# One store of 128 partitions in place of two of 64, in a fused attention and mixture-layer kernel

## The chip, the core and the metric

The kernel runs on one core of a Trainium2 chip. The metric is device time in microseconds (us), the median of several executions. Beside the times there is one profiled execution with its trace, from which all durations below are taken. The names of the engines are those of the profile: PE is the matrix engine, PEld its weight loads, DVE, ACT and POOL the vector, scalar and general engines, SP an engine that only issues transfers (DMAs). "SPq", "ACTq" and "POOLq" are the queues from which transfers are issued.

## The reference

Two layers follow each other; both work on float32.

```python
# attention without softmax, 8 batches, 8 heads, 576 tokens, 64 wide
kv  = einsum('bhsd,bhse->bhde', k, v)
o   = einsum('bhsd,bhde->bhse', q, kv)
o   = o / sqrt(mean(o * o, axis=-1) + 1e-6) * g_norm
x   = o.transpose(0, 2, 1, 3).reshape(8 * 576, 512)      # 4608 tokens

# feed-forward, 512 -> 1024 -> 512
h    = x @ w_in
u    = h * softmax(h, axis=-1)
ln   = (u - mean(u)) / sqrt(var(u) + 1e-6) * g_ln         # over the 1024
out  = ln @ w_out                                         # 4608 x 512 float32
```

The output is 4608 rows of 512 float32, which is 2 KB a row and 9.44 MB in all.

## The kernel before

**Tokens.** The kernel counts the 576 tokens of a batch as 9p + j, with p from 0 to 63 and j from 0 to 8. A chunk is 512 tokens. Chunk c (0 to 7) holds j = 0 to 7 of batch c, and the ninth chunk, number 8 (`LAST`), holds j = 8 of all eight batches. A result of 128 tokens is one block m (0 to 3) of a chunk: two values of j, each with its 64 values of p. So block m of chunk c stands in an SBUF tile of 128 partitions, where partitions 0 to 63 belong to one j and 64 to 127 to another, and in memory its rows are two runs of 64 rows, each with a step of nine rows. The step between the two runs is two rows. For the ninth chunk all 128 rows of a block have the same step of nine rows.

**Stages of a chunk.** `kv_mm` (L369) forms k^T v of a batch. `o_mm` (L434) multiplies it with the turned q. For chunks 0 to 4 PE turns q (L416), and for chunks 5 to 8 a transposing DMA on the SP queue does it (`q_turn`, L425, tile `qT_sb`). ACT and DVE then form the normalised x (L521). `h` is x times w_in, on PE: L574 for chunks 0 to 3 and L603 for chunks 4 to 8, in which the tokens lie along the partitions. ACT takes the exponential, DVE forms u. For chunks 4 to 8 u is turned by two transposing DMAs per chunk, each for two blocks, again on the SP queue (`ht_turn`, L639, tile `w_sb`). `out_mm` (L751) multiplies with w_out into a PSUM bank of 128 x 512, `scale` (L757) multiplies by the reciprocal deviation into the tile `ob_sb` on DVE (L244) or ACT (L242), and `store` (L762) writes `ob_sb` to memory.

**The store.** For chunks 0 to 7, `store` issues two transfers for a block, one for each half of the partitions (L769): 64 partitions of 2 KB, 128 KB each. For the ninth chunk it issues one transfer of 128 partitions for a block, and two of half the columns for the last block (L765). The stores of chunks 0 to 7 are all issued from SP. Those of the ninth chunk come from ACT and SP.

**Buffers and order.** The order of all the work is written out by hand in `ORDER` (L20); each engine runs its own part of it in that order. There are four `ob_sb` buffers in rotation (`kept`, L209), so the scale of a block waits until the store of the block four before it has landed. On SP the order from 57 us on is the stores of chunk 0, the qT transpose of chunk 5, the stores of chunk 1, that of chunk 6, the stores of chunk 2, that of chunk 7, and then stores mixed with the ten `w_sb` transposes. Loads of q, k, v and the weights are issued from POOL (all that have the kind "software_dynamic" in the profile), except for the first three and three short rows of norm weights (L297, L299: one of 8 rows, two of one row), which SP issues. Every transfer from SP or ACT also signals one of eight semaphores in turn, and waits until the transfer that used it before has landed.

Of the kernel before, what the change touches and what calls it, by code (L numbers as in the profile page):

```python
# [177 lines left out]
def kernel(  # L178
# [14 lines left out]
    B, H, S, D = q.shape  # L193
# [35 lines left out]
    on = {"act": nc.scalar, "dve": nc.vector, "pool": nc.gpsimd, "sp": nc.sync}  # L229
# [426 lines left out]
    for c in [c for c in range(NC) if c not in TOKS]:  # L656
        for f in range(NF):
# [9 lines left out]
            if f % 4 == 3 and c in PAIRED:  # L667
                m = f // 4
# [93 lines left out]
    def store(engine, c, m, cols):  # L762
        t = T["ob", c, m]
        if c == LAST:
            on[engine].dma_start(out.rearrange("(r j) d -> j r d", j=9)[8, 128 * m:128 * m + 128, cols], t[:, cols])  # L765
            return
        for x in range(2):
            j = 2 * (2 * (m % 2) + x) + m // 2
            on[engine].dma_start(  # L769
                out[c * S:c * S + S, :].rearrange("(p j) d -> j p d", j=9)[j], t[64 * x:64 * x + 64, :]  # L770
            )

    all_cols = slice(0, d_model)
    for c in range(NC):
        for m in range(4):
            key = ("out", c, m)
            if (c, m) == (LAST, 3):
                for x in range(2):
                    cols, half = slice(x * d_model // 2, (x + 1) * d_model // 2), (*key, x)
                    add(("out", c, m, x), "pe", lambda _, half=half, cols=cols: out_mm(half, range(NF), cols),  # L780
                        [("w_center", f) for f in range(NF)] + ([("turnu", c, m // 2)] if c in TOKS else [("u", c, f) for f in range(NF)]),
                        [("w" if c in TOKS else "u", c), half])
                    add(("ob", c, m, x), "dve|act", lambda e, half=half, cols=cols: scale(e, half, cols),
                        [("out", c, m, x), ("rstd", c)], [half, ("ob", c, m), ("rstd", c)])
                    add(("store", c, m, x), "sp|act", lambda e, c=c, m=m, cols=cols: store(e, c, m, cols), [("ob", c, m, x)], [("ob", c, m)])
                continue
            n_parts = 4 if c == 0 else 2
            for part in range(n_parts):
                fs = range(part * NF // n_parts, (part + 1) * NF // n_parts)
                add(("out", c, m, part), "pe", lambda _, key=key, fs=fs: out_mm(key, fs, all_cols),  # L790
                    [("w_center", f) for f in fs] + ([("turnu", c, m // 2)] if c in TOKS else [("u", c, f) for f in fs])
                    + ([("out", c, m, part - 1)] if part else []), [("w" if c in TOKS else "u", c), key])
            add(("ob", c, m), "dve|act", lambda e, key=key: scale(e, key, all_cols), [("out", c, m, n_parts - 1), ("rstd", c)], [key, ("ob", c, m), ("rstd", c)])
            add(("store", c, m), "sp|act" if c == LAST else "sp", lambda e, c=c, m=m: store(e, c, m, all_cols), [("ob", c, m)], [("ob", c, m)])
# [54 lines left out]
```

## Time and profile before

| what | value |
|---|---|
| median of 3 executions | 187.71 us (187.10 to 187.97) |
| the profiled execution's own time | 188.43 us |
| its span on the core | 186.7 us |
| PE busy | 171.0 us (92%) |
| ACT busy | 143.7 us (77%) |
| DVE busy | 134.9 us (72%) |
| POOL busy | 73.2 us (39%) |
| queue of the POOL loads (q0), share of 16 DMA engines | 50.2% |
| queue of the SP transfers (q1), share of 16 DMA engines | 43.0% |
| stores of L769 | 64 issues, 0.59 us each on SP (median), first at 56.9 us, last at 179.6 us |
| granted clock of PE | 0.997 |

The span runs from the first to the last instruction of the core; the execution's own time is 1.7 us more. The queues' shares add up the time that each packet took over all 16 DMA engines. A DMA engine can have packets of two queues in hand at once, so the shares of a stretch can add up to more than one. "Idle" is only of interest on the engine or queue that ends last in its stage.

### The profile page before, as it was taken

How to read it: one execution, taken by the hardware profiler on the slowest of the kernel's cores; microseconds unless marked ns; L12 is line 12 of the kernel's file. 1: busy time of each engine (PE TensorE's matmuls, PEld its weight loads, DVE VectorE, ACT ScalarE, POOL GpSimd, SP SyncE). 2: the span in 40 equal slices, each digit the busy share in tenths (PEclk: the TensorE clock that was granted, in tenths of full speed). 3: DMA queues.
4: the chain of work that ended last, by engine and by line, in shares of the span. 5: the costliest groups of instructions: out<-in, count | busy, mean ns of one | idle time of the engine just before them, and what ended most of it. 6: DMA issues, size and time to landing. Idle time of an engine off the chain costs nothing.

```text
span 186.7 us, 4938 instructions
## 1 busy us (share of the span) xinstructions
PE 171.0 (92%) x1985; PEld 84.6 (45%) x2007; DVE 134.9 (72%) x280; ACT 143.7 (77%) x282; POOL 73.2 (39%) x88
## 2 busy tenths in 40 slices
PE   7968899799999999999967899999999999999890
PEld 5455354255454464444523454444444444444350
DVE  1035567998648976878448968999898899999500
ACT  2437899889788999899968799898989869572351
POOL 7743049998599693998970200000000000000000
PEclk9999999999999999999999999999999999999998
DMA  5999999999999999939969974965979672959994
GB/s 203 284 207 210 207 338 283 210 205 209 208 210 206 274 236 150 205 66 163 222 178 137 285 135 87 202 135 112 210 151 191 122 177 59 211 124 199 188 237 168
DMA packets 50139, 35.48 MB, mean 190 GB/s; under 512 B 31548, under 2 KB 43332, under 8 KB 50116
## 3 DMA queue, kind: packets, MB, share of 16 engines
q0 software_dynamic: 13552, 16.42, 50.2%
q1 hardware_dynamic: 36132, 18.10, 43.0%
q10 hardware_dynamic: 432, 0.66, 1.0%
q8 instruction: 15, 0.25, 0.5%
q14 instruction: 8, 0.07, 0.1%
HBM read 32.51 MB, written 9.44 MB: 225 GB/s over the span
## 4 chain that ended last, share of the span: by engine, by line
PE 55%; DMA 26%; POOL 6%; ACT 4%; DVE 3%; issue 3%; SPq 1%; ACTq 0%; POOLq 0%
PE out_ps L751 25%; PE h_ps L603 13%; DMA w_in_sb<-in_moe_w_in_dram 8%; PE h_ps L574 7%; DMA q_sb<-in_q_dram 5%; DMA v_sb<-in_v_dram 5%; DMA qT_sb<-q_sb 4%; DMA w_sb<-u_sb 3%; PE s_ps L501 3%; PE misc_ps L685 2%; ACT e_sb L581 2%; PE o_ps L443 2%; PE misc_ps L378 2%; PE misc_ps L416 2%; DMA out_dram<-ob_sb 1%
## 5 line engine op out<-in xcount | busy, mean ns | idle before, releaser
L603 PE MATMUL h_ps<-w_in_sb,x_sb 128*128 128x512 bf16 x153 | 37.8, 379 | 0.5 <-issue 0.2
L751 PE MATMUL out_ps<-w_out_sb,w_sb 128*128 128x512 bf16 (+1 forms) x166 | 37.3, 369 | 0.6 <-DMA w_sb<-u_sb 0.4
L611 ACT ACTIVATE e_sb<-h_ps,zero_t 128x512 f32<-128x512 f32 x40 | 27.2, 682 | 8.2 <-PE h_ps L603 7.6
L521 DVE SCALAR_TENSOR_TENSOR x_sb<-o_ps,g_cols,rst_sb 128x512 bf16<-128x512 f32 x36 | 26.5, 746 | 9.2 <-ACT rst_sb L509 7.6
L751 PE MATMUL out_ps<-w_out_sb,u_sb 128*128 128x512 bf16 x122 | 30.8, 379 | 2.0 <-ACT lss_sb L505 1.7
L574 PE MATMUL h_ps<-x_sb,w_in_sb 128*128 128x512 bf16 x122 | 31.2, 380 | 1.4 <-DMA w_in_sb<-in_moe_w_in_dram 0.5
L238 POOL TENSOR_TENSOR usq_sb<-u_sb 128x512 bf16<-128x512 bf16 x27 | 27.4, 1040 | 9.7 <-DVE u_sb L585 9.7
L617 DVE TENSOR_TENSOR u_sb<-h_ps,e_sb 128x512 bf16<-128x512 f32 x40 | 26.8, 683 | 2.0 <-ACT e_sb L611 1.8
L623 DVE BATCH_NORM_STATS2 bn_sb<-u_sb 128x6 f32<-128x512 bf16 x40 | 26.6, 685 | 0.4
L236 ACT ACTIVATE osq_sb<-o_ps,zero_t 128x512 bf16<-128x512 f32 x36 | 23.2, 688 | 4.3 <-PE o_ps L443 4.1
L585 DVE TENSOR_TENSOR u_sb<-h_ps,e_sb 128x512 bf16<-128x512 f32 x32 | 21.4, 687 | 6.5 <-ACT e_sb L581 6.2
L505 ACT ACTIVATE lss_sb<-s_ps,eps_t 128x512 f32<-128x512 f32 x32 | 21.9, 688 | 4.0 <-PE s_ps L501 3.7
L751 PEld LDWEIGHTS <-w_sb 128*128 128x128 bf16 x168 | 16.1, 98 | 19.1 <-DMA w_sb<-u_sb 1.5
L603 PEld LDWEIGHTS <-x_sb 128*128 128x128 bf16 x160 | 15.3, 98 | 18.7 <-issue 0.4
L509 ACT ACTIVATE rst_sb<-lss_sb,zero_t 128x512 f32<-128x512 f32 x32 | 23.0, 722 | 0.6
L581 ACT ACTIVATE e_sb<-h_ps,zero_t 128x512 f32<-128x512 f32 x32 | 21.3, 689 | 2.7 <-PE h_ps L574 2.5
L598 POOL TENSOR_TENSOR es_sb<-e_sb 128x512 bf16<-128x512 f32 x16 | 20.2, 1276 | 5.5 <-ACT e_sb L581 5.3
L242 ACT ACTIVATE ob_sb<-out_ps,rstd_sb 128x512 f32<-128x512 f32 (+1 forms) x18 | 11.6, 661 | 10.3 <-PE out_ps L751 5.8
L751 PEld LDWEIGHTS <-u_sb 128*128 128x128 bf16 x128 | 12.1, 98 | 15.8 <-issue 2.5
L574 PEld LDWEIGHTS <-w_in_sb 128*128 128x128 bf16 x128 | 11.3, 97 | 15.7 <-issue 2.7
L244 DVE TENSOR_SCALAR ob_sb<-out_ps,rstd_sb 128x512 f32<-128x512 f32 x19 | 14.0, 744 | 5.2 <-ACT rstd_sb L708 2.0
L501 PE MATMUL s_ps<-osq_sb,head_mean 128*128 128x512 bf16 x35 | 13.1, 380 | 0.5 <-DVE u_sb L585 0.3
(72 smaller groups left out, 159.6 us busy)
## 6 DMA issues: line engine op xcount, KB each, us to landing
out_dram<-ob_sb SPq DMA_DIRECT2D x65, 128.0 KB, 2.7
k_sb<-in_k_dram POOLq DMA_DIRECT2D x6, 576.0 KB, 10.2
v_sb<-in_v_dram POOLq DMA_DIRECT2D x6, 576.0 KB, 10.6
q_sb<-in_q_dram POOLq DMA_DIRECT2D x6, 576.0 KB, 10.7
w_sb<-in_moe_w_out_dram POOLq DMA_DIRECT2D x2, 1024.0 KB, 15.5
w_in_sb<-in_moe_w_in_dram POOLq DMA_DIRECT2D x2, 512.0 KB, 13.9
v_sb<-in_v_dram POOLq DMA_DIRECT2D x3, 288.0 KB, 11.2
q_sb<-in_q_dram POOLq DMA_DIRECT2D x3, 288.0 KB, 10.5
```

What stands on the lines that cost most here:

```text
L236: nc.scalar.activation(out=dst, in_=src, func=AF.Square, bias=zero_t[:, :])
L238: on[engine].tensor_tensor(out=dst, in0=src, in1=src, op=MUL)
L505: nc.scalar.activation(out=t[:, :], in_=T["s", i][:, :], func=AF.Ln, bias=eps_t[:, :])
L509: nc.scalar.activation(out=t.rearrange("p a b c -> p (a b c)"), in_=T["lss", i][:, :], func=AF.Exp, scale=-0.5, bias=zero_t[:, :])
L521: nc.vector.scalar_tensor_tensor(out=t[:, 2 * hf:2 * hf + 2, z], in0=T["o", c, hf, z][:, :, :, :], scalar=g_rep, in1=T["rst", (c, hf, z)][ ...
L574: nc.tensor.matmul(bank(("h", c, f), [128, 512])[:, :], w_in_sb[:, dt, f * 128:(f + 1) * 128], T["x", c][:, dt].rearrange("p a b c -> p (a ...
L581: nc.scalar.activation(out=t[:, f % 2, :], in_=T["h", c, f][:, :], func=AF.Exp, bias=zero_t[:, :])
L603: nc.tensor.matmul(bank(("h", c, m, g), [128, 512])[:, :], x[:, NP * (m ^ 2 * odd(c, dt)) + dt, :] if c in TOKA else x[:, dt, m // 2 ^ odd ...
L611: nc.scalar.activation(out=t[:, g, :], in_=T["h", c, m, g][:, :], func=AF.Exp, bias=zero_t[:, :], accum_out=se[:, m, g:g + 1])
L617: nc.vector.tensor_tensor(out=t[:, m, g * 512:(g + 1) * 512], in0=T["h", c, m, g][:, :], in1=T["e", c, m][:, g, :], op=MUL)
L623: nc.vector.bn_stats(out=t[:, m, g, :], in_=T["u", c][:, m, g * 512:(g + 1) * 512])
L751: nc.tensor.matmul(bank(key, [128, d_model])[:, cols], T["w", c][:, m, f, :] if c in TOKS else T["u", c][:, f, m * 128:(m + 1) * 128], w_o ...
```

## The change

For chunks 0 to 7, `store` issues one transfer of all 128 partitions of `ob_sb` for a block. The target is described with three dimensions: two runs (step of two rows), 64 rows (step of nine rows), and 512 columns. The two transfers of 64 partitions are gone. The same bytes go to the same places, in rows of 2 KB as before.

```diff
         if c == LAST:
             on[engine].dma_start(out.rearrange("(r j) d -> j r d", j=9)[8, 128 * m:128 * m + 128, cols], t[:, cols])
             return
-        for x in range(2):
-            j = 2 * (2 * (m % 2) + x) + m // 2
-            on[engine].dma_start(
-                out[c * S:c * S + S, :].rearrange("(p j) d -> j p d", j=9)[j], t[64 * x:64 * x + 64, :]
-            )
+        first = 4 * (m % 2) + m // 2
+        on[engine].dma_start(out[c * S:c * S + S, :].rearrange("(p j) d -> j p d", j=9)[first:first + 3:2], t[:, :])
```

In the built program SP has 32 transfers with the pattern 2x64x512 on the side of the target (and 128 rows of 512 on the side of the tile) where it had 64 of 64x512 on both sides. The order of the work on PE, DVE, ACT and POOL is the same. The eight semaphores are handed round over 32 fewer transfers, so some instructions wait on a semaphore of another number, and the scale of a block waits for one store where it waited for two.

## The prediction

> **What bounds the kernel now.** I read the page first: busy time, queues, and the chain that ended last.
>
> ```profile
> span 186.7 us, 4938 instructions
> PE 171.0 (92%) x1985; PEld 84.6 (45%) x2007; DVE 134.9 (72%) x280; ACT 143.7 (77%) x282; POOL 73.2 (39%) x88
> ...
> q0 software_dynamic: 13552, 16.42, 50.2%
> q1 hardware_dynamic: 36132, 18.10, 43.0%
> ...
> PE 55%; DMA 26%; POOL 6%; ACT 4%; DVE 3%; issue 3%; SPq 1%; ACTq 0%; POOLq 0%
> ```
>
> PE bounds: 92% busy and over half of the chain. The stores are hardly on it. In the chain in order of time they appear in two places: two issues ahead of a transpose, and the last ones, for whose buffers ACT waits.
>
> ```profile
> 116.83 0.45 SPq L769
> 117.28 0.05 issue
> 117.33 0.59 SPq L769
> 117.92 0.05 issue
> 117.97 5.40 DMA w_sb<-u_sb
> ...
> 176.57 0.38 SPq L769
> 177.01 0.59 SPq L769
> 177.69 0.55 SPq L769
> 178.29 2.59 DMA out_dram<-ob_sb
> ```
>
> So stores are cheap as long as 16 DMA engines share them. How many share one is the question here, and the queue view, asked by stretch, answers it for three shapes. From 0 to 57 us, ahead of the first store's packets, SP's queue has moved three loads of 128 rows in two runs (256 packets each), one of 8 rows and two of one row:
>
> ```profile
> q1 hardware_dynamic: 836, 1.77, 9.0%
> ```
>
> 836 = 3 x (256 + 16) + (8 + 8) + 2 x (1 + 1): a completion record from each of 16 engines for the 128 rows, from 8 for the 8 rows, from one for the single row, although that row has 64 elements that could have been split. From 57 to 70 us the same queue has only the eight half stores of chunk 0:
>
> ```profile
> q1 hardware_dynamic: 640, 1.05, 25.1%
> ```
>
> 640 = 8 x (64 + 16): 64 rows go over 16 engines, four rows each. In every row the outermost dimension is what gets shared out, and an engine takes no part if that dimension has nothing for it.
>
> **The change part by part.** *Sharing out.* The 32 new transfers have 128 rows on the tile's side and 2x64x512 on the target's. The outermost dimension of the target has two entries. No row of before has sides that differ, so the bounds are 16 engines (the tile's side decides) and 2 (the target's side). I take 2, as the row of one row of 64 elements is nearest: what lies inside the outermost dimension was not split to fill engines. The Trainium skill, page "DMA: Bandwidth & Descriptors", section "Why a DMA increments its semaphore by 16 and not by 1", states the same: the number of engines is the largest up to 16 that divides the slowest dimension of both sides, here 2. The trace agrees for 128, 64, 8 and 1. The same page's section "Rules for kernel authors" also says that two transfers on the two halves of the partitions should be one of 128 partitions; that speaks for the change, and by it alone the time would be that of the first rival below.
>
> *Price of a store on two engines.* Each carries 64 packets of 2 KB, 131 KB. Prices of an engine, from the queue view: the ninth chunk's stores from ACT (128 partitions, all engines), 175 to 186.7 us; the half stores with no other traffic, 150 to 155 us; one `w_sb` transpose, 110 to 115 us; in that order:
>
> ```profile
> q10 hardware_dynamic: 432, 0.66, 15.7%
> ...
> q1 hardware_dynamic: 493, 0.81, 74.0%
> ...
> q1 hardware_dynamic: 2080, 0.52, 54.3%
> ```
>
> The first: 0.157 x 16 x 11.7 = 29.4 us for 0.66 MB, 22 GB/s an engine, 5.9 us for 131 KB; 1 KB packets and completions are in that, and its 2 KB packets alone have a median of 84 ns in the trace, 64 x 84 = 5.4 us. The second: 0.740 x 16 x 5 = 59.2 us for 0.81 MB, 13.7 GB/s, 9.6 us (148 ns a packet). Beside loads the same half stores ran at 0.251 x 16 x 13 = 52.2 us for 1.05 MB, 20 GB/s. So 148 ns appears where all 16 engines read the same 64 partitions at once; taken as pairs in each other's way it is 74 ns each, 4.7 us a store, the low bound. With two engines, each on its own half, the ninth chunk's row is nearest: 5.4 us; bounds 4.7 and 9.6. A half store now holds an engine for 4 x 84 to 4 x 148 = 0.3 to 0.6 us.
>
> *Sum on one of the two engines, from the first store at 57 us.* Stores: 32 x 5.4 = 172.8. Transposes, all after 57 us and on all engines: 0.543 x 5 = 2.7 us for one of 16 blocks; ten of `w_sb` and one of `q_last` are 29.7, three of 18 blocks are 3 x 3.05 = 9.2; together 38.9. Loads: from 57 us to the end q0 has 25.7% of 129.7 us = 33.3 us of packet time per engine; in 57 to 80 us packet times overlapped to a share of 1.15, so 29. Ninth chunk: 1.05 MB over 16 engines, 32 packets x 84 = 2.7. Sum 243.4, so the two engines are through at 300.4, where the whole kernel ends at 186.7 now. This work was hidden behind PE, which has some 120 us of its own in that time; it is no cover any more.
>
> *Does the queue stay full?* Loads and stores share the engine packet by packet: four stores of chunk 0 (21.6) and the loads up to q of chunk 5 (three queued and five still to be issued, 8 x 2.8 = 22: one is 576 KB, at the 208 GB/s of the page's slices around 45 us) fill 57 to about 101 us. That load landed at 82.7 before (SP issued the transpose then), so qT of chunk 5 is some 20 us late; PE, which follows its order, waits at `kv_mm` and `o_mm`. SP issues in order: stores of chunk 1 behind that transpose, 104 to 126; qT of chunk 6 (before 95.0), about 129; stores of chunk 2 to about 154 with the last loads; qT of chunk 7 (before 105.5) and the first `w_sb` transpose (before 110.1) at about 157; and so on, each transpose behind up to four stores, 22 us. A block's scale (0.74 us) needs the store four before it landed; while three others still hold the engine for 16 us, the next is ready in time. So I let the queue run without gaps, at nothing. If each of the 14 transposes left it dry for the 1.8 us from issue to first packet (2.4 to landing, less 0.6 of packets), that would be 25 us; and if SP's waits for q loads (26.6 us before) were not filled, 27 more.
>
> *The end.* The last scale waits for chunk 7's last store to land: two halves 0.84, issue 0.45, landing 2.5 = 3.8 us. Span 304.2.
>
> *SP's issues.* 32 fewer of 0.59 us take 19 us off SP, worth nothing while the engines are the queue; in the chain shown they would be worth about one 0.59 before the transpose and one at the end. No other engine's order moves, and no load.
>
> Span 304.2 plus the 1.7 us outside it is 306; the profiled execution is 0.7 us above the median of the runs, so **305 us**.
>
> **The rivals.** *First, the other side: all 16 engines take part.* Then there are 8 packets an engine at 84 ns (0.67) for two halves of 4 x 148 (1.18). The chain gains 0.6 at the transpose at 117 us, 0.6 of issue and 0.5 of packets at the end: 188.4 - 1.7 = 186.7, against the median 186.0. It decides if the tile's 128 rows, not the target's 2 runs, are what is shared out. For it: 128 rows went over 16 engines in the loads, whose tile side looks the same. Against: their memory side began with 128 too.
>
> *Second, two engines at the slow pace:* 32 x (9.6 - 5.4) = 134 more, 439. Against: two engines on separate halves have no partner on their partitions.
>
> *Third, two engines, but a lone engine overlaps its packets,* so that 84 ns is twice what it costs: 32 x 2.7 = 86 less, 219. Against: from 2 to 5 us SP's loads fill 96.5% of 16 engines at 1.06 MB, 22.9 GB/s an engine, so packets of one queue follow each other, not over each other. Up to 1.15 of overlap with the loads and transposes is inside my range.
>
> *Fourth, two engines with gaps:* 305 + 25 = 330, or 357 with the unfilled waits.
>
> **How the numbers follow.** The forecast with smaller or larger gaps (254 to 357) has 0.78, the first rival 0.11 (0.08 faster, 0.02 within 0.5%, 0.01 slower), the second 0.05, the third 0.06. Low end: 4.7 us a store takes 22 off, 283; overlap of 1.15 on what is left takes (283 - 57) x 0.13 = 29 more, 254. High end: the fourth rival, 357. Faster 0.08, same 0.02, slower 0.90; 0.5%, or 0.9 us, is about what this kernel's times can tell.
>
> **What would show it.** Packets: 32 x (128 + 2) = 4160 of stores instead of 64 x 80 = 5120, so some 960 fewer than 50139 with two engines; 32 x 144 = 4608 and 512 fewer with sixteen. The median landing of a store rises from 2.7 us to 15 to 24. The chain turns from PE to DMA `out_dram` and `w_sb`, PE's busy time stays near 171 us of a longer span, and the DMA share from 110 us on falls to some 0.3, since 14 engines have only transposes. The step "two engines" is wrong if the landing stays under 4 us; the price is wrong if stores follow each other at other than 5.4 us; "no gaps" is wrong if the DMA view has stretches with nothing in hand.

## The result, and the profile after

The changed kernel takes 298.61 us (median of four executions, 298.24 to 299.15) against 187.41 us of the kernel before on the same chip (187.08 to 187.97): a ratio of 1.593, 95% interval 1.588 to 1.598. The profiled execution took 298.44 us, of which the span is 296.0. Some executions of five of the experiments below ran slower, at a lower granted clock of PE, and are left out of the times; for the kernel with stores from POOL that leaves one execution, and the trace is of a slower one.

The packets of the page before, and the head of the page of the changed kernel, with the granted clock of PE and the busy share of the DMA engines in 40 slices, the two queues with their packets, megabytes and share of 16 engines, and the chain that ended last:

```profile
DMA packets 50139, 35.48 MB, mean 190 GB/s; under 512 B 31548, under 2 KB 43332, under 8 KB 50116
```

```profile
span 296.0 us, 4893 instructions
PE 193.8 (65%) x1985; PEld 89.7 (30%) x2007; DVE 135.9 (46%) x280; ACT 144.0 (49%) x282; POOL 73.3 (25%) x88
...
PEclk9999999999857599859966959989977968557955
DMA  7999999997919333971585939769611961983221
...
DMA packets 49178, 35.47 MB, mean 120 GB/s; under 512 B 30588, under 2 KB 42372, under 8 KB 49156
q1 hardware_dynamic: 35172, 18.09, 41.3%
q0 software_dynamic: 13552, 16.42, 33.1%
...
DMA 63%; PE 17%; SPq 7%; ACT 4%; DVE 3%; POOL 2%; issue 2%; DVEq 0%; POOLq 0%; ACTq 0%
```

The bound has moved from PE to the transfers. PE is idle for a third of the span, and the chain is 63% DMA, the larger part of it `out_dram`. The other engines have their busy times of before; that of PE rose, to which the part on the prediction comes back. The packets say how the stores are shared out: 50139 - 49178 = 961 fewer. Two engines per store make 32 x (64 x 2 + 2) = 4160 records where there were 64 x (64 + 16) = 5120, 960 fewer; sixteen would have made 512 fewer. In queue 1 alone, which carries these stores, it is 36132 - 35172 = 960; the other packet is one of queue 14, which has no stores.

Where the time is lost shows in the chain in order of time. The pieces of 8 us and more from 57 us on, with their start and duration:

```profile
69.31 29.64 DMA out_dram<-ob_sb
...
104.43 25.16 DMA out_dram<-ob_sb
...
146.51 8.06 SPq L425
...
158.22 13.96 DMA w_sb<-u_sb
...
177.32 13.05 DMA qT_sb<-q_last
...
194.80 12.48 DMA out_dram<-ob_sb
...
210.33 28.35 DMA out_dram<-ob_sb x2
...
242.13 17.37 DMA out_dram<-ob_sb
...
267.12 24.85 DMA out_dram<-ob_sb x2
```

A piece of `out_dram` runs from the issue of a store to its landing ("x2" joins two); 25 to 30 us of it is a store that lands behind the others of its group. The transposes between them (`w_sb`, `qT_sb`) are in the chain with 13 to 14 us, where the first `w_sb` transpose in the chain of before has 5.4: they stand behind stores. "SPq L425" is the issue of a transpose that holds SP, with 8 us of it in the chain.

The queue view of a stretch in which only stores run, 215 to 225 us (GB/s of the core in 40 slices, then packets and queue 1):

```profile
GB/s 49 49 49 57 49 49 57 49 49 49 49 49 57 49 49 57 49 49 49 49 57 49 49 57 49 49 49 49 57 49 49 57 49 49 49 49 57 49 49 57
DMA packets 254, 0.51 MB, mean 51 GB/s; under 512 B 4, under 2 KB 4, under 8 KB 254
...
q1 hardware_dynamic: 254, 0.51, 13.1%
```

13.1% of 16 engines is 2.1: two engines are busy without a gap and fourteen do nothing. 250 packets of 2 KB in 10 us on two engines are one per engine in 80 ns, so a store of 64 packets on each takes 5.1 us.

### The profile page after: what moved, and what is told of

Its sections match the earlier page's. It is cut to its first block, busy times and chain, and to the rows that moved or that the text cites. A ratio compares the mean times of both kernels' runs of the same rounds, so it can differ in the third digit from the quotient of the medians.

```text
span 296.0 us, 4893 instructions
## 1 busy us (share of the span) xinstructions
PE 193.8 (65%) x1985; PEld 89.7 (30%) x2007; DVE 135.9 (46%) x280; ACT 144.0 (49%) x282; POOL 73.3 (25%) x88
## 2 busy tenths in 40 slices
DMA packets 49178, 35.47 MB, mean 120 GB/s; under 512 B 30588, under 2 KB 42372, under 8 KB 49156
## 3 DMA queue, kind: packets, MB, share of 16 engines
q1 hardware_dynamic: 35172, 18.09, 41.3%
q0 software_dynamic: 13552, 16.42, 33.1%
## 4 chain that ended last, share of the span: by engine, by line
DMA 63%; PE 17%; SPq 7%; ACT 4%; DVE 3%; POOL 2%; issue 2%; DVEq 0%; POOLq 0%; ACTq 0%
DMA out_dram<-ob_sb 47%; PE out_ps L751 5%; DMA w_sb<-u_sb 5%; DMA w_in_sb<-in_moe_w_in_dram 5%; DMA qT_sb<-q_last 4%; PE h_ps L574 4%; DMA v_sb<-in_v_dram 3%; SPq L639 3%; PE h_ps L603 3%; SPq L425 3%; SPq L768 2%; DVE ob_sb L244 1%; ACT e_sb L581 1%; PE misc_ps L378 1%; PE s_ps L501 1%
## 5 line engine op out<-in xcount | busy, mean ns | idle before, releaser
L751 PE MATMUL out_ps<-w_out_sb,w_sb 128*128 128x512 bf16 (+1 forms) x166 | 47.6, 438 | 32.2 <-DMA w_sb<-u_sb 26.1
L603 PE MATMUL h_ps<-w_in_sb,x_sb 128*128 128x512 bf16 x153 | 45.2, 436 | 8.6 <-DVE u_sb L617 7.4
L574 PE MATMUL h_ps<-x_sb,w_in_sb 128*128 128x512 bf16 x122 | 33.3, 401 | 9.9 <-DVE ob_sb L244 8.6
L751 PEld LDWEIGHTS <-w_sb 128*128 128x128 bf16 x168 | 18.3, 112 | 58.4 <-DMA w_sb<-u_sb 28.4
L751 PE MATMUL out_ps<-w_out_sb,u_sb 128*128 128x512 bf16 x122 | 33.1, 401 | 0.5 <-issue 0.2
L603 PEld LDWEIGHTS <-x_sb 128*128 128x128 bf16 x160 | 17.2, 109 | 44.0 <-issue 30.9
L521 DVE SCALAR_TENSOR_TENSOR x_sb<-o_ps,g_cols,rst_sb 128x512 bf16<-128x512 f32 x36 | 26.5, 745 | 6.9 <-ACT rst_sb L509 5.3
L443 PE MATMUL o_ps<-qT_sb,kvd 64*64 64x256 bf16 (+1 forms) x192 | 8.0, 262 | 22.3 <-DMA qT_sb<-q_sb 9.4
```

Source lines behind the costliest of these rows:

```text
L521: nc.vector.scalar_tensor_tensor(out=t[:, 2 * hf:2 * hf + 2, z], in0=T["o", c, hf, z][:, :, :, :], scalar=g_rep, in1=T["rst", (c, hf, z)][ ...
L574: nc.tensor.matmul(bank(("h", c, f), [128, 512])[:, :], w_in_sb[:, dt, f * 128:(f + 1) * 128], T["x", c][:, dt].rearrange("p a b c -> p (a ...
L603: nc.tensor.matmul(bank(("h", c, m, g), [128, 512])[:, :], x[:, NP * (m ^ 2 * odd(c, dt)) + dt, :] if c in TOKA else x[:, dt, m // 2 ^ odd ...
L751: nc.tensor.matmul(bank(key, [128, d_model])[:, cols], T["w", c][:, m, f, :] if c in TOKS else T["u", c][:, f, m * 128:(m + 1) * 128], w_o ...
```

## The experiments

**Is it the number of engines, and is it the outermost dimension that sets it?** The theory: the number of DMA engines is the largest divisor, up to 16, of the outermost dimension. The rival: something else in a store of 128 partitions, or fewer and larger transfers. Both kernels keep stores of 64 partitions with plain two-dimensional patterns, and cut each into two pieces. They differ by two rows in the place of the cut. Against the changed kernel, whose two lines of the store go:

```diff
-        ...
+        for x in range(2):
+            j = 2 * (2 * (m % 2) + x) + m // 2
+            rows = out[c * S:c * S + S, :].rearrange("(p j) d -> j p d", j=9)[j]
+            for lo, hi in ((0, 62), (62, 64)):        # e3; e4: ((0, 60), (60, 64))
+                on[engine].dma_start(rows[lo:hi], t[64 * x + lo:64 * x + hi, :])
```

Cut 62 + 2:

> The kernel before with each half store of 64 rows cut in 62 and 2 rows, patterns of two dimensions throughout. Theory (the number of engines is the largest divisor up to 16 of the outermost count): 62 and 2 both go on two engines, 31 + 1 packets an engine a half, 64 a block as in the changed kernel: 290 to 310 us. Rival (rows are dealt out over 16 engines, four each, whatever the count): 187 to 195 us, with 128 issues on SP as the only cost.

Cut 60 + 4:

> The control for 62 and 2: each half store cut in 60 and 4 rows, the same 128 transfers. Theory of the largest divisor: 15 and 4 engines, 5 packets on the fullest engine a half where there were 4: 188 to 196 us. If the cutting itself or 128 issues were what costs, it would be as slow as 62 and 2.

Measured, with two executions each: 306.53 us for 62 + 2 (ratio to before 1.635, 1.625 to 1.645) and 193.14 us for 60 + 4 (1.030, 1.023 to 1.038), both as the theory expected. The packets of the page, 62 + 2 first:

```profile
DMA packets 49371, 35.48 MB, mean 117 GB/s; under 512 B 30780, under 2 KB 42564, under 8 KB 49348
...
DMA 52%; SPq 21%; PE 14%; DVE 3%; ACT 3%; POOL 3%; issue 2%; DVEq 0%; POOLq 0%; ACTq 0%
```

and 60 + 4:

```profile
DMA packets 50331, 35.49 MB, mean 185 GB/s; under 512 B 31740, under 2 KB 43524, under 8 KB 50308
...
PE 57%; DMA 20%; DVE 6%; ACT 5%; POOL 4%; SPq 4%; issue 2%; ACTq 0%; DVEq 0%; POOLq 0%
```

62 rows on two engines and 2 on two make 64 x (62 + 2) + 64 x (2 + 2) = 4352 records, 768 fewer than the 5120 of before: 50139 - 49371 = 768. 60 rows on 15 engines and 4 on four make 64 x (60 + 15) + 64 x (4 + 4) = 5312, 192 more: 50331 - 50139 = 192. Both have 128 issues where before has 64, the same halves, rows and bytes; two rows in the cut make a difference of 113 us. So the cause is the number of engines, and it goes by divisors: 62 rows go over two engines, not 16 or 15, though every row is a packet of its own. This is the rule of the Trainium skill, page "DMA: Bandwidth & Descriptors", section "Why a DMA increments its semaphore by 16 and not by 1"; the packets of this case agree with it for 64, 62, 60, 4 and 2.

**What would one store of 128 partitions cost if all 16 engines took part?** The first rival of the prediction was that. It can be had if the two sides of the transfer are laid out alike. In the first pair, the product that forms x (L521) writes the tokens of a block in another order, (p, j) in place of (j, p), so that a block is 32 values of p with four of j each; the outermost dimension is 32. The other kernel of the pair has the same order and stores two halves of 16 x 4 rows.

```diff
-        nc.vector.scalar_tensor_tensor(out=t[:, 2 * hf:2 * hf + 2, z], ...)
+        for n in range(2) ...:
+            to = t[:, 2 * hf:2 * hf + 2, z][:, n]
+            to = to.rearrange("p y e -> p (y e)").rearrange("p (e y) -> p y e", y=4)
+            nc.vector.scalar_tensor_tensor(out=to, in0=T["o", c, hf, z][:, n], ...)
...
+        rows = out[c * S:c * S + S, :].rearrange("(p j) d -> p j d", j=9)[32 * (m % 2):32 * (m % 2) + 32]
+        on[engine].dma_start(rows[:, m // 2:m // 2 + 7:2], t[:, :])                        # e1
+        on[engine].dma_start(rows[16 * x:16 * x + 16, m // 2:m // 2 + 7:2], t[64 * x:64 * x + 64, :])   # e2, x = 0, 1
```

> The tokens of a block are laid down in another order (32 values of p, each with four j), so that one store of 128 partitions has 32x4x512 on the memory side in place of 2x64x512: still one transfer of 128 partitions, three dimensions, rows of 2 KB, but an outermost count of 32. For that the x multiply of DVE is issued as two halves. Theory (the outermost count sets the number of engines): 16 engines, 16 completion records a store, landing near 2.7 us, and a time of 186 to 188 us. Rival (a pattern of three dimensions, or one transfer per block, is itself what is slow): stays near 298 us.

> The order of tokens as in the run with 32x4x512, but each block stored as two transfers of 64 partitions (16x4x512 each). Theory: 16 engines as well, 187 to 189 us. The difference to the run with one transfer is the price of two issues in place of one with all else equal: my first rival put it at 1.7 us. If it is under 0.5 us, the two half stores cost nothing on the path.

Measured: 191.45 us with one store (ratio 1.021, 1.018 to 1.025) and 192.48 with two (1.026, 1.021 to 1.031), some 3.5 us above both expectations, but far from the rival's 298. The stores of the first, with issue times and landing, and its packets:

```profile
L771 SPq DMA_DIRECT2D out_dram<-ob_sb x32: 538/562/936, 59.6 to 182.2; - x32
DMA to landing us min/median/max: 1.7/2.6/9.3
...
DMA packets 49627, 35.48 MB, mean 186 GB/s; under 512 B 31036, under 2 KB 42820, under 8 KB 49604
```

50139 - 49627 = 512 fewer: sixteen engines, with a three-dimensional target and 128 partitions in one transfer, as in the changed kernel. What the change does badly is thus not the merging and not the third dimension, but that this dimension is two and is the outermost. Both kernels are 2% slower than before, the one with two stores a block too, which points at what they share, the new order: the product that forms x, in the line's row by tile,

```profile
L525 DVE SCALAR_TENSOR_TENSOR x_sb<-o_ps,g_cols,rst_sb x68: 732/780/812, 16.0 to 161.2; 128x256 bf16<-128x256 f32 x64, 128x512 bf16<-128x512 f32 x4
```

costs 780 ns for 256 columns, where it cost 750 for 512: a half written with a step is no cheaper than a whole. With 32 more such instructions (the 28 in an expectation below is a slip) DVE's busy time goes from 134.9 to 150.6 us, and its share of the chain from 3% to 17% (26% with two stores). That this is all of the 2% is not shown.

So a second pair moved the order elsewhere, to PE, which reads the turned q with a step; the stores are as in the first pair:

```diff
...
-                            qT[rows, slice(first, first + 4) if c < B else first + y, 64 * hh:64 * hh + 64],
+                            qT[rows, first:first + 4, 64 * hh:64 * hh + 64].rearrange("k y e -> k e y") if c < B else
+                            qT[rows, first + y, 64 * hh:64 * hh + 64],
```

> The inner order of tokens again (32x4x512 on the memory side, one store a block), but made where PE reads the turned q (the 256 columns of the second attention product are read in the order p, j), so that DVE keeps its 36 x multiplies of 0.75 us. Theory: the run with 32x4x512 lost 3.5 us against the kernel before to 28 more DVE instructions and 15.7 us more of DVE, not to its stores. If PE reads the other order at the same pace, 185.5 to 187.5 us, which is 0 to 1.7 us under before. If it reads at half the pace, the product's 256-column instructions cost up to 6 us more on PE: 188 to 194 us.

> The same reading order on PE with two stores of 64 partitions a block (16x4x512). Against the run with one store it prices two issues for one with all else equal: 1.7 us by my first rival, about 1 us by the first pair of runs, nothing if the difference of that pair was noise.

Measured: 191.64 us with one store of 128 partitions and 192.16 with two, both at a ratio of 1.022 (1.016 to 1.027), the first within the 188 to 194 expected if PE read at half the pace. In the row of the product, PE pays for the step:

```profile
L443 PE MATMUL o_ps<-qT_sb,kvd x192: 192/597/608, 12.0 to 145.0; 64*64 64x256 bf16 x128, 64*64 64x64 bf16 x64
```

The median was 269 ns before. For the question asked, the two pairs agree: 1.0 and 0.5 us between two stores and one on the same 16 engines, with overlapping intervals. So the gain of 1.7 us that the first rival promised is not shown; whether it is nothing or about 1 us stays open, and a layout that costs less than that was not found.

**Does the time follow the packets?** Each of the 32 stores writes the first 256 columns only; columns 256 to 511 of chunks 0 to 7 are left out of the output. The packets are 1 KB, their number is the same.

```diff
-        on[engine].dma_start(out[...].rearrange("(p j) d -> j p d", j=9)[first:first + 3:2], t[:, :])
+        on[engine].dma_start(out[...].rearrange("(p j) d -> j p d", j=9)[first:first + 3:2, :, 0:256], t[:, 0:256])
```

> The changed kernel, but the stores of chunks 0 to 7 write only columns 0 to 255 (1 KB a row); the other half of those rows is left out. As many packets, half the bytes. Theory (the pace of two engines' packets): the ninth chunk's 1 KB packets took 46 ns, so 32 x 64 x 46 = 94 us where 2 KB packets took 164: 298.6 - 70 = 229 us, within 215 to 240. Rival (the number of packets or the holding of SP sets it): near 298 us.

Measured: 222.46 us in two executions (ratio 1.187, 1.176 to 1.198), within the 215 to 240 expected; the page has 49178 packets again, 31.28 MB. A packet of 1 KB follows the one before in 43 ns where stores run alone (up to 47 packets in 1 us on two engines), against 80 for 2 KB. So a store goes with its bytes, at 24 to 26 GB/s an engine, with little per packet. The 32 x 64 packets at 37 ns less are 76 us, and 298.6 - 222.5 = 76.1. That it fits so closely is in part luck, since PE has 46% of the chain again here and DMA 40%.

**Is there a share of such stores that costs nothing?** The sum of the prediction, with the prices measured, is 57 us to the first store, 5.1 for each store on two engines, 0.67 to 1.18 for each of the others (2 x 4 packets at 84 to 148 ns), 71 for transposes, loads and the ninth chunk, and 4.0 + 2.4 to the end. For no such store that is 156 to 172, well under the 187 that PE sets; for 8 it is 191 to 203, little above PE's time. The theory was that the time is the larger of the two; the rival, that each long store also delays the transposes behind it.

```diff
+        if m == 0:                       # e5, 8 stores;  e6, 16 stores: m % 2 == 0;  e8, 20 stores: c >= 3
             first = 4 * (m % 2) + m // 2
             on[engine].dma_start(out[...].rearrange("(p j) d -> j p d", j=9)[first:first + 3:2], t[:, :])
+            return
+        for x in range(2):               # the others as before, two of 64 partitions
```

> Only block 0 of each chunk (8 of 32) is stored as 2x64x512, the others as two halves as before. Theory (two engines are a queue of their own that binds only when its work passes PE's): 57 + 8 x 5.1 + 48 x 0.45 + 69 of transposes, loads and ninth chunk + 5.5 at the end = 195 us, within 188 to 205. Rival (a fixed price for each such store, (298.6 - 187.4) / 32 = 3.5 us): 187.4 + 8 x 3.5 = 215 us.

> Blocks 0 and 2 of each chunk (16 of 32) as 2x64x512. Theory of the two engines' queue: 57 + 16 x 5.1 + 32 x 0.45 + 69 + 5.5 = 228 us, within 215 to 238. Rival of the fixed price: 187.4 + 16 x 3.5 = 243 us.

> The stores of chunks 3 to 7 (20 of 32) as 2x64x512 from SP, those of chunks 0 to 2 as two halves. Two engines' queue from 115 us on: 20 x 5.1 = 102, 12 transposes 32, ninth chunk 3, end 5.5: 115 + 142.5 = 258 us, within 240 to 270. It is the control for the same stores from POOL.

| stores on two engines | the sum, us | measured, us | over before | per store |
|---|---|---|---|---|
| 8 (one per chunk) | 191 to 203 | 207.2 and 208.7 | 20.6 | 2.6 |
| 16 (two per chunk) | 227 to 235 | 233.4 | 46.0 | 2.9 |
| 20 (all of chunks 3 to 7) | 244 to 251 | 255.3 | 67.9 | 3.4 |
| 32 | 298 | 298.6 | 111.2 | 3.5 |

("Over before" is over 187.4 us throughout.) The ratios with intervals are 1.245 (1.239 to 1.251) for 16 and 1.369 (1.359 to 1.378) for 20, from two executions each; for 8 it is 208.0 over 187.4, 1.11, from two executions as well. From 16 on the sum describes the time within some us (in the last row it must, since the 71 us were taken from there), and the expectations of the two engines' queue for 16 and 20 hold, while the rival's 243 for 16 fails. With 8 it falls short by 5 to 17 us: both expectations fail, 195 as too low and the rival's 215 as too high. What such a store costs where the two engines are not full is seen in the chain of the kernel with 8:

```profile
89.83 9.19 DMA out_dram<-ob_sb
99.02 8.45 DMA qT_sb<-q_sb
...
121.83 10.01 DMA w_sb<-u_sb
...
186.74 2.15 SPq L639
...
191.80 8.38 DMA out_dram<-ob_sb
```

In the chain of before this `qT_sb` has

```profile
94.96 8.01 DMA qT_sb<-q_sb
```

and there are 5.40 us for `w_sb` at 117.97 and 2.59 for the last `out_dram` at 178.29. PE goes on behind the transpose at 107.5 where it went on at 103.0 (4.5 us later), behind the first `w_sb` at 131.9 where it was 123.4 (8.5 later); and at the end the last store adds 8.38 - 2.59 = 5.8 to the 13.5 that have gathered by then (191.8 against 178.3). Of the 2048 data packets of that `w_sb` transpose some 470 go before 126 us, nearly all of them between 124.5 and 125.5, beside the store; from 126 to 128 none goes, and the others go from 128.5 on, when the store's are through. (A packet does not name its engine, so that the early ones are on the fourteen engines without a store is inferred.) PE is 92% busy before, so what it waits there is lost. Nothing in these runs is a free share.

**Would it help to take the stores out of the transposes' queue?** Two kernels, with the stores issued from another engine. The first is the kernel with 20 stores, these issued from POOL (in the order written out by hand, `store.3.3` becomes `store.3.3:pool`, and so on):

> The same 20 stores as 2x64x512, issued from POOL, which has no other work after 106 us but two copies. If a transfer from POOL also goes on the same two engines: near 258 us. If POOL's transfers are spread otherwise (all 16 engines, or another pair each time), no pair has more than a few of them: 187 to 200 us. It tells apart that a store is on two engines (slow to land, 5.1 us of packets) from that all of them are on the same two.

Measured: 217.6 us, in one execution; the traced one took 227.1. The answer is neither of the two: better than from SP (255.3) by 38 us, not back at 187 to 200. The issue rows, with the median from issue to landing, and queue 0 from 165 to 175 us, when it has only these stores:

```profile
out_dram<-ob_sb POOLq DMA_DIRECT2D x20, 256.0 KB, 11.4
```

```profile
GB/s 17 17 17 18 35 52 69 68 85 134 133 199 165 133 149 117 164 98 66 131 115 132 82 115 131 98 115 66 100 66 98 66 66 49 99 67 66 99 115 99
...
q0 software_dynamic: 1465, 0.91, 41.4%
```

Up to 199 GB/s, where SP's stores alone ran at 49 to 57: 41.4% of 16 is 6.6 engines. Queue 0 has 24112 packets where before it has 13552: 10560 more, 528 for each store, which the trace shows as 64 packets of 4 KB, two rows each, 448 small ones of 8 bytes and 16 completions. So from POOL the same pattern is not held to the same two engines, and several stores run side by side. This says nothing against the two engines of SP's queue; it is another way to issue. A store still takes 11.4 us to land, against 2.7 before; whether that is what keeps this kernel from 187 to 200 us was not tested.

The second is the kernel with 8 stores, issued from ACT (`store.0.0:act` and so on). The theory by then: behind the store in one queue a transpose waits out its 5 us; from another queue it would share the two engines with it and be late by less.

> Block 0 of each chunk as 2x64x512 (8 of 32), but these eight issued from ACT, whose queue is another than SP's. Theory as mended after the dose of 8 (207 to 209 us undisturbed, where the engines' sum gave 195): PE has no slack, and a transpose that stands behind a two-engine store in SP's queue comes 5 us late; out of that queue the transposes share the two engines packet by packet and lose little: 190 to 200 us. Rival (the two engines' time itself is what costs): 205 to 212 us, as from SP.

Measured: 215.7 us (215.4 to 216.9; ratio 1.149, 1.142 to 1.157): slower than from SP (208.0), and outside both expectations. The three largest pieces of the chain after 57 us are transposes again:

```profile
95.29 16.25 DMA qT_sb<-q_sb
...
127.04 10.68 DMA w_sb<-u_sb
...
186.50 15.95 DMA w_sb<-u_sb
```

The queue view of this kernel from 194 to 198 us, where the transpose is in queue 1 and the store in queue 10 (ACT):

```profile
GB/s 28 23 49 46 82 79 87 82 123 77 82 87 79 97 87 113 108 82 84 79 84 82 82 79 84 82 82 79 100 84 97 100 110 84 79 84 82 82 79 84
...
q1 hardware_dynamic: 632, 0.16, 106.5%
q10 hardware_dynamic: 84, 0.17, 10.8%
```

From 186.0 to 187.2 us the transpose ahead of this one ran alone, at 205 to 228 GB/s. Beside the store, queue 1 moves 632 packets in 4 us, 158 in 1 us; a transpose alone in before moves its 2080 in 2.6 us, 800 in 1 us or one in 20 ns on each engine. All 16 engines show packets in hand all the time (106.5%), though 14 of them have nothing else to do. An engine that takes a 2 KB packet (80 ns) and a transposing one (20) in turn does one of each in 0.1 us; 16 engines at that pace do 160 in 1 us, which is what is measured; the store's 84 packets in the 4 us are one in 95 ns on each of its two engines. These rates fit a transpose that moves at the pace of its slowest engine, on all of them. To share two engines with a store then costs it more than to stand behind it: PE goes on behind the `qT_sb` at 111.5 us, against 107.5 with the stores issued from SP, and behind the first `w_sb` of the chain at 137.7, against 131.9. That the engines are held in step is inferred from these rates; how, no run here tells.

## Why the prediction came out as it did

The time predicted was 305 us, the time measured is 298.6, inside the range and on the side that had 0.90. Step by step:

- **Two engines.** Right: 961 fewer packets against 960, and the runs with 62 and 60 rows show that it is the outermost dimension's divisors that decide. The first rival is ruled out for this change. The row of one row of 64 elements, which the choice between two and sixteen rested on, was the right neighbour. The rule that the prediction takes from the Trainium skill, page "DMA: Bandwidth & Descriptors", section "Why a DMA increments its semaphore by 16 and not by 1", speaks there of the slowest dimension that is not of size 1; for such a row that could be read as its 64 elements, which would mean 16 engines, while the packets show one. For 2x64x512 both readings give two.
- **Price of a store.** 5.4 us was taken; 80 ns a packet make 5.1, so 32 stores are 164 us in place of 172.8. The second rival (148 ns a packet) and the third (42) both fall. This term, 8.8 us too large, is the whole miss of the sum (304.2 against a span of 296.0); the other terms were too small by 0.6 together.
- **The rest on the two engines.** Transposes, loads and the ninth chunk were put at 70.6 us. The last store landed at 292.0, so 292.0 - 57 - 164 = 71 us went to the rest and to gaps together. The agreement is of the sum alone, and partly luck: pauses of the queue may be in it against loads that cost less. In the packets of all engines together, pauses of over 0.2 us in which none starts add up to 6.0 us between 57 and 292; pauses of the two engines alone can't be told apart. The sharing with the loads was right in kind: from 61 to 91 us, beside loads, 336 packets of stores go in 30 us, 11 in 1 us, where alone 25 do.
- **"No gaps".** It holds roughly. In stretches of stores alone there is none, and the fourth rival's 330 was not reached. Chunk by chunk it went otherwise than written: the qT transpose of chunk 5 came at 92.4 us, 10 later than before, where 20 were forecast; SP began to issue the next two at 118.1 and 140.7 us, where 129 and 157 were forecast, but each issue then held SP for 12.6 and 13.9 us, until the stores ahead of it were through (their packets end near 129 and 154). So SP's issues, costed at nothing, are in the chain with 7%. It costs little here, because the two engines have work meanwhile.
- **The end.** 3.8 us forecast, 292.0 to 296.0 measured; outside the span 2.4 against 1.7.
- **What was to be seen.** Three signs were forecast wrongly. PE's busy time did not stay near 171 us but rose to 193.8, with a granted clock of 0.835 in place of 0.997; in the last 36 us, where PE is busy 37% of the time, the clock is 0.64. It weighs little here, where PE has 17% of the chain. The DMA share did not fall to 0.3; it is 0.59 to 0.78 between 57 and 260 us, because a packet of a waiting transpose counts as in hand for as long as it waits: of the 0.71 from 110 to 260 us, 0.31 are 135 packets of 256 bytes that took 0.5 to 7.6 us each, where half of such packets take 18 ns. Only where stores run alone, 0.13, does the share tell the number of engines. And the page gives no landing for the new stores, so their median can't be read; in the chain the first two pieces of `out_dram`, of one store each, have 29.6 and 25.2 us, beyond the 15 to 24.

The columns of the view by stretch are the busy times of PE, its weight loads, DVE, ACT and POOL with their counts, then granted clock, DMA share and GB/s. In the changed kernel:

```profile
57.00:104.00 47.00, 29.08 (x489) 13.85 (x493) 21.29 (x44) 24.81 (x46) 21.43 (x22) 0.78 0.76 124
...
192.00:225.00 33.00, 26.05 (x131) 10.86 (x132) 19.54 (x42) 18.92 (x42) 0.00 (x0) 0.86 0.59 86
225.00:260.00 35.00, 18.01 (x67) 7.19 (x67) 14.44 (x30) 7.67 (x19) 0.00 (x0) 0.79 0.74 80
260.00:296.00 36.00, 13.43 (x44) 5.37 (x44) 2.30 (x10) 4.07 (x8) 0.00 (x0) 0.64 0.37 86
```

And the waits, in us in total, times, and the longest: the scale of a block waits for the store four before it, and `out_mm` for the turned u.

```profile
ACT ob_sb L242 <- DMA out_dram<-ob_sb: 52.1, 10, 17.0
DVE ob_sb L244 <- DMA out_dram<-ob_sb: 49.9, 10, 9.5
...
PE out_ps L751 <- DMA w_sb<-u_sb: 26.1, 4, 11.1
```

One thing the good fit hides. The prediction took the time as the work of the busiest resource, and that is right where the two engines hardly stop, from 16 stores on. With 8 stores the sum gives at most 203 us and the kernel takes 208; what is missing in it there is the path: long stores stand ahead of transposes that PE waits for.

## What to carry to other kernels

Before two transfers are made one, look at the outermost dimension on both sides: in SP's queue here the number of DMA engines was its largest divisor up to 16 (of the 2 where the sides had 128 and 2), and a dimension of 2 (or of 62) meant two engines, 5.1 us a store and 1.59 times the kernel's time, while the same bytes with an outermost 32 kept all 16. The packet count of the profile tells the number of engines, since each engine adds a completion record to each transfer. Below the point where a sum of work binds, ask what stands in the queue behind each long transfer.

## What the runs showed of the hardware that was not expected

- A DMA transpose beside a store on two engines was slow on all 16: 158 packets in 1 us against 800 alone, and 16.25 us in the chain for a `qT_sb` that has 8.01 before.
- SP, which only issues, was held by a transpose queued behind stores for up to 13.9 us (1.8 to 3.2 before).
- PE's granted clock and its busy share went down together: 0.997 at 92% before, 0.974 at 85% with 8 such stores, 0.927 at 79% with 16, 0.835 at 65% with 32. What sets the clock was not tested.
- Issued from POOL, a target of 2x64 rows was cut into packets of 4 KB and not held to two engines.
- PE took 597 ns for 256 columns read with a step, 269 without; DVE took 780 ns for 256 columns written with a step, 750 for 512 without.
